# Second routing of a two-layer MoE chain: expert logits from four column strips of the array and one product with a 0-1 matrix

## The chip, the core and the metric

One NeuronCore of a Trainium2 chip runs the whole program. The metric is the device time of one execution in microseconds (us), less is better. The engines are TensorE (PE; its weight loads are listed as PEld), VectorE (DVE), ScalarE (ACT), GpSimd (POOL) and SyncE (SP, which here only issues DMAs). Each engine works through its own queue in program order.

## The reference, cut to what matters

```python
def reference(...):
    attn_out = _attn_ref(q, k, v)               # decaying linear attention, 2 x 8 heads x 768 tokens x 64
    x = attn_out.transpose(0, 2, 1, 3).reshape(1536, 512)
    x = _moe_ref(x, w_skip, w_gate, w1, w2)     # tokens with x @ w_skip > 0 go to 1 of 8 experts
    return _moe2_ref(x, w_gate2, w1b, w2b, capacity)

def _moe2_ref(x, w_gate, w1, w2, capacity):
    logits = x @ w_gate                         # 1536 x 8
    expert_idx = np.argmax(logits, axis=1)
    ...                                         # place of each token within its expert, softmax gate
    h = np.maximum(np.einsum('ecd,edf->ecf', disp, w1), 0.0)
    y = np.einsum('ecf,efd->ecd', h, w2)
    ...                                         # out[i] = gate_w[i] * y[expert_idx[i], pos[i]]
```

All data are float32; there are 1536 tokens of 512 features, 8 experts and 1024 hidden features in both MoE layers.

## The kernel before, in words

The program has three stages on the same core: the attention with the routing of the first MoE, the first MoE with the routing of the second, and the second MoE. A block is 128 tokens on 128 partitions; 512 features are four parts (`KT` = 4) of 128. An expert's weights come in four chunks of 1 MB (two of layer 1, two of layer 2) through `load_w`; `prep` makes of each chunk a rounded copy `hi` on ACT (L236, a copy of 128x2048) and a remainder `lo` on DVE (L244). A product with such weights (`mm3`, L680 to L682) is three matmuls, hi x hi, hi x lo and lo x hi.

The order of the work in the second stage is written out by hand. The loop at L827 goes over the experts e. In each turn there are `layer1` of expert e (24 matmuls of 512 columns), the turning of the next block x (`split_T`, four transposes at L673, then L383 on ACT and L384 on DVE), `layer2` of expert e-1 (24 matmuls) and the turning of the hidden block h (eight transposes). The generators yield after every six matmuls and after every four transposes. At each yield `run` calls `step_side`, which lets every side generator do its next piece; so one turn has eleven side steps. `prep` is called at four places in a turn: at its start, in the middle of `layer1` (right after the relu of its first half, L696 to L698), after the turning of x, and in the middle of `layer2`.

`route_b` (L713) is the side generator that routes the finished block of expert e-1 for the second MoE. `then_route` starts it after `layer2` with a number of idle steps ahead (`lead`) and a number of idle steps after the logits (`rest`). Its pieces are:

- start: the new rows `r2` on DVE (L716), and some small ones (L721, L723)
- with lead 3, at the second side step of the next turn (in the middle of the next `layer1`): four transposes (L731) into a PSUM bank, and a copy of 128x512 by ACT into `x2t` (L733)
- one step later: `token_logits` (L248), four products with the feature part of `x2t` as the 128-column weights and 8 gate columns of `idw` as the moving side; then `pick` (L284: a chain of eight small DVE operations from L289 to L309, with Exp on ACT, L296), the write of the rows to the table by a DMA on POOL's queue (L344), and `mrow` (L741) on DVE
- `1 + rest` steps later: `ranked` (two bf16 products), `prb`, `slb`, `hotb` (L746, L748, L378) and `cumb` on DVE
- one step later: one product of `hotb` and `mrow` (L758) and the sum into `idb` (L759); for e = 6 also the gather of the first block of the second MoE and `load_held`

The steps on ACT around it, in program order, are: L733, the relu of the first half of `layer1` (L696), `hi` of a weight chunk (L236), Exp (L296), the relu of the second half (L696), `xh` of the next block (L383), the next `hi`.

`then_route` is called for the blocks 0 to 5 with lead 3 and rest 3, for block 6 with lead 3 and rest 1, and for block 7 (the last, with no loop turn behind it) with lead 0 and rest 1. `idw[:, g, :]` holds, of feature parts 2g and 2g+1, the 17 gate columns of the odd part in columns 0 to 16, a 128x128 identity in 17 to 144, and the 17 gate columns of the even part in 145 to 161; the second MoE's gate columns are the entries 8 to 15 of the 17. `psum()` gives one of three banks by turns. `constants` (L127) sets up small constants on POOL before the second chunk of the attention.

```python
        x2t = m_p.tile([128, KT, 128], F32, tag="x2t", name="x2t", bufs=1)
        nc.scalar.activation(out=x2t, in_=xr.rearrange("p (k t) -> p k t", k=KT), func=ACTF.Copy)
        yield
        lp = psum()
        token_logits(lp, lambda k: x2t[:, k, :], 8, 8)
        m = pick(lp[:, 0:8].unsqueeze(1), 1, 1, rm, ...)[:, 0, :]
```

Of the kernel before, what the change touches and what calls it, by code (L numbers as in the profile page):

```python
# [7 lines left out]
F32 = mybir.dt.float32  # L8
# [3 lines left out]
ACTF = mybir.ActivationFunctionType  # L12
ALU = mybir.AluOpType
# [3 lines left out]
NT, DM, E, FF = B * S, H * D, 8, 1024  # L17
NCH = S // 128
NTILE = NT // 128
KT = DM // 128  # L20
# [13 lines left out]
C_ID = C_GS + 4 * NCH  # L34
# [11 lines left out]
def kernel(  # L46
# [12 lines left out]
    nc = tc.nc  # L59
    ctx.enter_context(tc.manual_schedule())  # L60
    const = ctx.enter_context(tc.tile_pool(name="const", bufs=1))
# [11 lines left out]
    def bank(name, *tags):  # L73

        i = turns[name] = turns.get(name, -1) + 1
        tag = tags[i % len(tags)]
        return ps.tile([128, 512], F32, tag=tag, bufs=BANKS[tag], name=name)
# [17 lines left out]
    cs = const.tile([128, C_N], F32, name="cs")  # L95
# [3 lines left out]
    idw = const.tile([128, 2, 164], F32, name="idw")  # L99
# [9 lines left out]
    iota = const.tile([128, 256], F32, name="iota")  # L109
    idacc = const.tile([128, 2, 16], F32, name="idacc")  # L110
    idb = const.tile([128, E], F32, name="idb")

    def no_rows():

        nc.sync.dma_start(out=table[0:1, :], in_=zb[0:1, :].bitcast(F32))
# [11 lines left out]
    def constants():  # L127
        nc.sync.dma_start(out=cs[:, C_ID:C_N], in_=cst[:, C_ID:C_N])
        wk = wg.rearrange("p (g i) n -> p g i n", i=2)
        nc.sync.dma_start(out=idw[:, :, 145:162], in_=wk[:, :, 0, 0:17])  # L130
        nc.sync.dma_start(out=idw[:, :, 0:17], in_=wk[:, :, 1, 0:17])
        nc.sync.dma_start(out=cap_i, in_=capacity.bitcast(I32))
        for t in t9.values():
            nc.gpsimd.memset(t, 0.5)
        for g in range(2):
            nc.gpsimd.tensor_copy(out=idw[:, g, 17:145], in_=cs[:, C_ID:C_ID + 128])
        nc.gpsimd.tensor_copy(out=lc, in_=cs[:, C_L:C_L + 256].rearrange("p (a t) -> p a t", a=2))
        nc.gpsimd.tensor_copy(out=iota[:, 0:128], in_=cs[:, C_IOTA:C_IOTA + 128])
        nc.gpsimd.tensor_scalar(out=iota[:, 128:256], in0=cs[:, C_IOTA:C_IOTA + 128], scalar1=128.0, scalar2=None, op0=ALU.add)
        nc.gpsimd.memset(cum, 0.0)  # L140
        nc.gpsimd.memset(cumb, 1.0)
        nc.gpsimd.memset(idacc, 0.0)
        nc.gpsimd.tensor_copy(out=cap, in_=cap_i[:, 0:1])
        for t in row2:
            nc.gpsimd.memset(t, 0.0)

    def idle(n):
        for _ in range(n):
            yield
# [39 lines left out]
    def load_held():  # L189

        held[1] = True
        for _ in range(held[0]):
            load_w()
# [54 lines left out]
    def token_logits(lp, xk, c0, n):  # L248

        for k in range(KT):  # L250
            w0 = c0 + (0 if k % 2 else 145)
            nc.tensor.matmul(out=lp[:, 0:n], lhsT=xk(k), rhs=idw[:, k // 2, w0:w0 + n], start=k == 0, stop=k == KT - 1)  # L252

    def xk(rows, k):

        return rows[:, KW * k:KW * k + 128]

    def x_all(rows):
        return rows.rearrange("p (k z) -> p k z", z=KW)[:, :, 0:128]
# [57 lines left out]
    def ranked(rk, lmat, m2d, cum2d):  # L317
        n = m2d.shape[-1]
        nc.tensor.matmul(out=rk[:, 0:n], lhsT=lmat, rhs=m2d, start=True, stop=False)
        nc.tensor.matmul(out=rk[:, 0:n], lhsT=ones, rhs=cum2d, start=False, stop=n < 32)  # L320
        if n == 32:
            nc.tensor.matmul(out=rk[:, 16:32], lhsT=ones, rhs=m2d[:, 0:16], start=False, stop=True)
# [15 lines left out]
    def write_rows(eng, src, n, c0=0, c1=RW):  # L338

        r0 = done[0]  # L340
        r1 = r0 + 128 * n
        if c1 == RW:
            done[0] = r1
        eng.dma_start(out=table[r0:r1, c0:c1].rearrange("(n p) w -> p n w", p=128), in_=src[:, :, c0:c1])  # L344
# [21 lines left out]
    def places(out, rank, m0):  # L366

        n = rank.shape[-1]
        sl = sm.tile([128, n], F32, tag=f"sl0{n}", name="sl0")
        nc.vector.scalar_tensor_tensor(out=sl, in0=m0, scalar=-AWAY, in1=rank, op0=ALU.mult, op1=ALU.add)  # L370
        for i in range(n):
            nc.vector.tensor_scalar(
                out=out[:, i, :], in0=iota[:, 0:128], scalar1=-AWAY, scalar2=sl[:, i:i + 1], op0=ALU.add, op1=ALU.is_equal
            )

    def slot_hot(out, rank):

        nc.vector.tensor_scalar(  # L378
            out=out, in0=iota[:, 0:out.shape[-1]], scalar1=rank, scalar2=None, op0=ALU.is_equal
        )  # L380
# [268 lines left out]
    def psum(name="t"):  # L649
        return bank("e" + name, *{"t": "a", "s": "cbb", "o": "d"}[name])  # L650
# [62 lines left out]
    def route_b(e, xs, acc, lead, rest):  # L713

        r2 = row2[e % 2]
        nc.vector.scalar_tensor_tensor(  # L716
            out=x_all(r2), in0=acc.rearrange("p (k t) -> p k t", k=KT), scalar=xs[:, GCOL:GCOL + 1], in1=x_all(xs),
            op0=ALU.mult, op1=ALU.add,
        )
        if xs is not r2:  # L720
            nc.vector.tensor_copy(out=r2[:, IDCOL:IDCOL + 1], in_=xs[:, IDCOL:IDCOL + 1])  # L721
        rm = sm.tile([128, 1, 8], F32, tag="rmb", name="rmb")
        nc.vector.scalar_tensor_tensor(  # L723
            out=rm, in0=xs[:, IDCOL:IDCOL + 1].unsqueeze(1).to_broadcast([128, 1, 8]), scalar=0.0, in1=rev.unsqueeze(1),
            op0=ALU.not_equal, op1=ALU.mult,
        )
        yield
        yield from idle(lead)
        xr = psum()
        for k in range(KT):  # L730
            nc.tensor.transpose(xr[:, 128 * k:128 * k + 128], xk(r2, k), ident)  # L731
        x2t = m_p.tile([128, KT, 128], F32, tag="x2t", name="x2t", bufs=1)
        nc.scalar.activation(out=x2t, in_=xr.rearrange("p (k t) -> p k t", k=KT), func=ACTF.Copy)  # L733
        yield
        lp = psum()
        token_logits(lp, lambda k: x2t[:, k, :], 8, 8)
        m = pick(lp[:, 0:8].unsqueeze(1), 1, 1, rm, r2[:, GCOL + 1:GCOL + 2].unsqueeze(1))[:, 0, :]
        write_rows(nc.gpsimd, r2.unsqueeze(1), 1)
        n = NTILE + e
        mrow = sm.tile([128, E], F32R, tag="mrowb", name="mrowb")  # L740
        nc.vector.tensor_scalar(out=mrow, in0=m, scalar1=cs[:, C_ROW + n:C_ROW + n + 1], scalar2=None, op0=ALU.mult)  # L741
        yield from idle(1 + rest)
        rk = psum()
        ranked(rk, lc[:, 1, :], m, cumb)
        pr = sm.tile([128, E], F32, tag="prb", name="prb")
        nc.vector.tensor_tensor(out=pr, in0=rk[:, 0:8], in1=m, op=ALU.mult)  # L746
        sl = sm.tile([128, 1], F32, tag="slb", name="slb")
        nc.vector.tensor_reduce(out=sl, in_=pr, axis=AX.X, op=ALU.add)  # L748
        hot = sm.tile([128, 128], F32R, tag="hotb", name="hotb", bufs=1)
        slot_hot(hot, sl)  # L750
        nc.vector.tensor_tensor(out=cumb, in0=cumb, in1=m, op=ALU.subtract)
        if e == E - 1:
            oh = sm.tile([128, 128], F32, tag="ohb", name="ohb", bufs=2)
            places(oh.unsqueeze(1), sl, m[:, 0:1])
            late.append((r2, oh))
        yield
        new = psum()
        nc.tensor.matmul(out=new[:, 0:E], lhsT=hot, rhs=mrow, start=True, stop=True)  # L758
        nc.vector.tensor_tensor(out=idb, in0=idb, in1=new[:, 0:E], op=ALU.add)  # L759
        if e == E - 2:  # L760
            late.append(gather(numbers(idb[:, 0:1], "id0"), 1 + NT + 128 * E - 128))
            load_held()
        yield
# [58 lines left out]
    def then_route(e, acc, lead, rest):  # L822
        g = route_b(e, xs1[e], acc, lead, rest)
        next(g)
        side.append(g)

    for e in range(E):  # L827
        if e > 1:
            prep()
        h = run(layer1(x, "w1a", e, prep))  # L830
        if e + 4 < E:
            xs1[e + 4] = gather(ida[:, e + 4:e + 5], 1 + NT)
        elif e == 4:
            gather(ida[:, 8:9], 1 + NT, a0)
        turn = split_T(h, FT, "hT")
        if e == 0:
            next(turn)
        x = run(split_T(xs1[e + 1] if e + 1 < E else a0, KT, "x"))
        prep()
        if e:  # L840
            acc = run(layer2(hT.pop(e - 1), "w2a", e - 1, prep))
            then_route(e - 1, acc, 3, 3 if e < E - 1 else 1)
        hT[e] = run(turn)
    prep()
    acc = run(layer2(hT.pop(E - 1), "w2a", E - 1, prep))
# [31 lines left out]
    acc = run(layer2(h0, "w2b", 0))  # L877
# [59 lines left out]
    acc = run(layer2(h0, "w2b", 0, prep))  # L937
# [202 lines left out]
```

## Time and profile before

| | |
|---|---|
| three runs, median (lowest to highest) | 396.01 us (395.87 to 396.07) |
| the profiled execution, its own time | 394.56 us |
| its span, first to last instruction | 392.8 us |
| PE busy | 376.2 us, 96% of the span, 2605 matmuls |
| DVE busy | 259.7 us, 66% |
| ACT busy | 215.6 us, 55% |
| POOL busy | 69.9 us, 18% |
| granted clock of TensorE, mean | 0.994 of full speed |

The second stage, with the code of the change, runs from about 80 to 208 us of the span. In the turn from 118.29 to 132.60 us PE is busy for 14.28 of 14.31 us, DVE for 13.30 and ACT for 10.79. The matmuls overlap in the records (a new one starts while the former still drains), so the cost of a group of matmuls is read from its start to the start of the next group, not from its busy time. One float32 product shows as two matmul records; a transpose and a product with a float32r operand as one. Instructions on ACT and DVE overlap by about 0.1 us in the same way.

### The profile page before, as it was taken

The page shows a single profiled execution, that of the slowest core. Times are in us where ns is not written, and L with a number is a line of the kernel's source. Part 1 is how long each engine was busy: PE and PEld are TensorE (multiplying, and loading weights), DVE is VectorE, ACT ScalarE, POOL GpSimd, SP SyncE. Part 2 cuts the span into 40 slices and gives each one's busy share as a digit, 9 for nine tenths or more (in the row PEclk, how much of TensorE's full clock was granted, in tenths as well). Part 3 has the DMA queues.
Part 4 walks back from the last instruction along what each step waited for, and adds up shares of the span by engine and source line. Part 5 has one row for each costly group of instructions (what it writes and reads, how often), then busy time and mean ns, then how long its engine had stood idle before and what let it go on. Part 6 is the DMA issues. An engine that isn't in the chain of part 4 may idle for free.

```text
span 392.8 us, 6614 instructions
## 1 busy us (share of the span) xinstructions
PE 376.2 (96%) x2605; PEld 321.0 (82%) x2605; DVE 259.7 (66%) x476; ACT 215.6 (55%) x283; POOL 69.9 (18%) x97
## 2 busy tenths in 40 slices
PE   8899989899999999999999999999999999999992
PEld 3788878678877877877778898989989899898981
DVE  2668986478898999999863868383574738455210
ACT  1557773296778777777543845545545555552201
POOL 6310010180031010000026020404013040301101
PEclk9999999999999999999999999999999999999997
DMA  8999993489999999889875587858575684320101
GB/s 304 402 419 417 379 333 120 131 298 385 391 351 336 343 357 316 323 319 300 333 260 159 180 283 236 279 164 306 168 230 191 224 288 136 130 62 7 47 2 41
DMA packets 18409, 97.69 MB, mean 249 GB/s; under 512 B 3263, under 2 KB 3391, under 8 KB 8900
## 3 DMA queue, kind: packets, MB, share of 16 engines
q1 hardware_dynamic: 12180, 80.03, 56.5%
q0 software_dynamic: 4000, 13.25, 10.1%
q10 hardware_dynamic: 2192, 3.93, 2.7%
q8 instruction: 22, 0.36, 0.3%
q14 instruction: 15, 0.12, 0.1%
HBM read 88.11 MB, written 10.14 MB: 250 GB/s over the span
## 4 chain that ended last, share of the span: by engine, by line
PE 71%; DVE 10%; issue 7%; ACT 6%; DMA 5%; POOL 1%; POOLq 0%; ACTq 0%; DVEq 0%
PE eo L680 10%; PE es L680 10%; PE es L682 10%; PE es L681 10%; PE eo L682 10%; PE eo L681 9%; DMA cs<-in_cst_dram 4%; DVE lo L244 3%; PE s L267 2%; PE et L673 2%; ACT hi L236 2%; DVE lo L228 2%; PE et L252 1%; PE et L890 1%; DMA a<-table,id 1%
## 5 line engine op out<-in xcount | busy, mean ns | idle before, releaser
L244 DVE TENSOR_TENSOR lo<-raw,hi 128x2048 fp32r<-128x2048 f32 x60 | 136.2, 2283 | 5.9 <-ACT hi L236 5.9
L236 ACT ACTIVATE hi<-raw 128x2048 fp32r<-128x2048 f32 x60 | 114.7, 1915 | 20.2 <-PE eo L682 15.4
L680 PE MATMUL eo<-hi,hTh 128*128 128x512 f32 x192 | 77.9, 406 | 0.2 <-ACT hTh L383 0.2
L682 PE MATMUL eo<-hi,hTl 128*128 128x512 f32 x192 | 75.5, 393 | 0.0
L681 PE MATMUL eo<-lo,hTh 128*128 128x512 f32 x192 | 75.0, 390 | 0.0
L682 PE MATMUL es<-xh,lo 128*128 128x256 f32 x224 | 62.9, 281 | 0.0
L680 PE MATMUL es<-xh,hi 128*128 128x256 f32 x224 | 62.9, 281 | 0.0
L681 PE MATMUL es<-xl,hi 128*128 128x256 f32 x224 | 62.9, 281 | 0.0
L910 DVE SCALAR_TENSOR_TENSOR hTl<-es,hTh 128x512 fp32r<-128x512 f32 x28 | 19.3, 691 | 63.1 <-ACT hTh L909 63.1
L325 POOL DMA_INDIRECT out_dram<-y,ixo x16 | 20.2, 1260 | 142.3 <-ACT y L767 129.5
L682 PEld LDWEIGHTS eo<-hi,hTl 128*128 128x128 f32 x192 | 36.0, 188 | 8.5 <-DVE hTl L384 0.5
L681 PEld LDWEIGHTS es<-xl,hi 128*128 128x128 f32 x224 | 42.7, 191 | 0.3
L680 PEld LDWEIGHTS es<-xh,hi 128*128 128x128 f32 x224 | 42.7, 190 | 0.3
L682 PEld LDWEIGHTS es<-xh,lo 128*128 128x128 f32 x224 | 42.7, 191 | 0.0
L680 PEld LDWEIGHTS eo<-hi,hTh 128*128 128x128 f32 x192 | 36.1, 188 | 6.9 <-ACT hTh L383 0.5
L681 PEld LDWEIGHTS eo<-lo,hTh 128*128 128x128 f32 x192 | 36.2, 188 | 6.8
L909 ACT ACTIVATE hTh<-es 128x512 fp32r<-128x512 f32 x28 | 16.7, 598 | 40.0 <-PE es L682 40.0
L680 PE MATMUL es<-hi,xh 128*128 128x512 f32 x80 | 33.4, 418 | 0.3 <-ACT xh L383 0.3
L682 PE MATMUL es<-hi,xl 128*128 128x512 f32 x80 | 31.6, 395 | 0.1
L681 PE MATMUL es<-lo,xh 128*128 128x512 f32 x80 | 31.3, 392 | 0.0
L767 ACT ACTIVATE y<-eo,xs 128x512 f32<-128x512 f32 x15 | 10.3, 688 | 33.0 <-PE eo L682 25.2
L540 DVE TENSOR_TENSOR p<-s,cs 128x512 f32<-128x512 f32 x24 | 15.4, 682 | 12.7 <-PE s L531 12.7
(153 smaller groups left out, 506.0 us busy)
## 6 DMA issues: line engine op xcount, KB each, us to landing
raw<-in_w1a_dram SPq DMA_DIRECT2D x16, 1024.0 KB, 7.0
raw<-in_w2a_dram SPq DMA_DIRECT2D x16, 1024.0 KB, 7.1
raw<-in_w1b_dram SPq DMA_DIRECT2D x16, 1024.0 KB, 5.2
raw<-in_w2b_dram SPq DMA_DIRECT2D x16, 1024.0 KB, 4.9
ain<-in_qkv_dram SPq DMA_DIRECT2D x10, 1024.0 KB, 10.1
table<-rowc ACTq DMA_DIRECT2D x5, 580.0 KB, 5.8
table<-row POOLq DMA_DIRECT2D x8, 290.0 KB, 6.6
ain<-in_qkv_dram SPq DMA_DIRECT2D x4, 512.0 KB, 5.8
```

The lines of the kernel that those rows point to most:

```text
L228: nc.vector.tensor_tensor(out=lo[:, k], in0=r3[:, k], in1=hi[:, k].bitcast(F32), op=ALU.subtract)
L236: nc.scalar.activation(out=hi, in_=r3, func=ACTF.Copy)
L244: nc.vector.tensor_tensor(out=lo, in0=r3, in1=hi.bitcast(F32), op=ALU.subtract)
L267: nc.tensor.matmul(out=t[:, 128 * i:128 * i + KW], lhsT=xt(2 * g + i), rhs=idw[:, g, 17 - 17 * i:17 - 17 * i + KW], start=i == 0, stop=i = ...
L325: return nc.gpsimd.indirect_dma_start(out=dst[:, :], out_offset=bass.IndirectOffsetOnAxis(ap=idx, axis=0), in_=src, in_offset=None, bounds ...
L540: nc.vector.tensor_tensor(out=t, in0=sa[j].rearrange("p (r t) -> p r t", r=4), in1=mask.unsqueeze(1).to_broadcast([128, 4, 128]), op=ALU.mult,
L680: nc.tensor.matmul(out=acc, lhsT=a[0], rhs=w[0], start=first, stop=False)
L681: nc.tensor.matmul(out=acc, lhsT=a[0], rhs=w[1], start=False, stop=False)
L682: nc.tensor.matmul(out=acc, lhsT=a[1], rhs=w[0], start=False, stop=last)
L767: nc.scalar.activation(out=y, in_=acc, func=ACTF.Copy, scale=xs[:, GCOL + 1:GCOL + 2])
L909: nc.scalar.activation(out=hi[:, g:g + 2, :], in_=acc, func=ACTF.Relu)
L910: nc.vector.scalar_tensor_tensor(out=lo[:, g:g + 2, :], in0=acc, scalar=0.0, in1=hi[:, g:g + 2, :].bitcast(F32), op0=ALU.max, op1=ALU.subtract
```

## The change

In `route_b`, for the blocks 0 to 6, the logits are made in another way. Each of the four feature parts gets its own product, with 32 columns of `idw` as the weights and the 128 tokens of `x2t` as the moving side; the outputs go to four strips of 32 partitions of one PSUM bank. The 32 columns start at 0 for an odd part and at 130 for an even one, so that they hold the 8 gate columns of the second MoE and other columns. ACT copies the 128x128 result over the first part of `x2t`, and after a further side step one product with this copy as weights and a 128x8 matrix `sel` as the moving side adds the four strips' gate rows and turns the result to tokens on partitions. `sel` is 1 where a row of the strips is gate row j; POOL builds it in `constants` from the identity. The idle steps after the logits are one fewer for the blocks 0 to 5. Block 7 keeps the old way.

```diff
+    sel = const.tile([128, E], F32, name="sel")
...
         nc.gpsimd.memset(idacc, 0.0)
+        nc.gpsimd.tensor_copy(out=sel, in_=cs[:, C_ID + 23:C_ID + 31])
+        for z in (40, 87, 104):
+            nc.gpsimd.tensor_tensor(out=sel, in0=sel, in1=cs[:, C_ID + z:C_ID + z + 8], op=ALU.add)
...
         yield
         lp = psum()
-        token_logits(lp, lambda k: x2t[:, k, :], 8, 8)
+        if e == E - 1:
+            token_logits(lp, lambda k: x2t[:, k, :], 8, 8)
+        else:
+            for k in range(KT):
+                w0 = 0 if k % 2 else 130
+                nc.tensor.matmul(
+                    out=lp[32 * k:32 * k + 32, 0:128], lhsT=idw[:, k // 2, w0:w0 + 32], rhs=x2t[:, k, :], start=True, stop=True
+                )
+            nc.scalar.activation(out=x2t[:, 0, :], in_=lp[:, 0:128], func=ACTF.Copy)
+            yield
+            lp = psum()
+            nc.tensor.matmul(out=lp[:, 0:8], lhsT=x2t[:, 0, :], rhs=sel, start=True, stop=True)
         m = pick(lp[:, 0:8].unsqueeze(1), 1, 1, rm, r2[:, GCOL + 1:GCOL + 2].unsqueeze(1))[:, 0, :]
...
-            then_route(e - 1, acc, 3, 3 if e < E - 1 else 1)
+            then_route(e - 1, acc, 3, 2 if e < E - 1 else 1)
```

## Rows read from the trace of the kernel before

**Rows 1.** Part 1 of the page: busy time, share of the span, instructions.

```profile
PE 376.2 (96%) x2605; PEld 321.0 (82%) x2605; DVE 259.7 (66%) x476; ACT 215.6 (55%) x283; POOL 69.9 (18%) x97
```

**Rows 2.** Timeline, PE, routing of block 1: start us, duration us, engine, line.

```profile
117.96 0.60 PE L731 MATMUL et<-cs,row 128*128 128x128 f32 x4
...
119.81 0.95 PE L252 MATMUL et<-idw,x2t 128*128 128x8 f32 x8
120.61 0.48 PE L680 MATMUL es<-hi,xh 128*128 128x512 f32 x1
...
122.11 0.60 PE L673 MATMUL et<-cs,xs 128*128 128x128 f32 x4
```

**Rows 3.** Timeline, ACT, the same stretch; idle time before and its releaser in brackets.

```profile
118.66 0.60 ACT L733 ACTIVATE x2t<-et 128x512 f32<-128x512 f32 x1 [0.86 <-PE et L731]
119.15 0.59 ACT L696 ACTIVATE h<-es 128x512 f32<-128x512 f32 x1
119.63 1.91 ACT L236 ACTIVATE hi<-raw 128x2048 fp32r<-128x2048 f32 x1
121.55 0.21 ACT L296 ACTIVATE ex<-d 128x8 f32<-128x8 f32 x1
122.31 0.60 ACT L696 ACTIVATE h<-es 128x512 f32<-128x512 f32 x1 [0.56 <-PE es L682]
```

**Rows 4.** Timeline, DVE, the same stretch, to the hot matrix of block 1.

```profile
121.15 0.16 DVE L289 TENSOR_REDUCE mx<-et 128x1 f32<-128x8 f32 x1
...
122.48 0.21 DVE L741 TENSOR_SCALAR mrowb<-m,cs 128x8 fp32r<-128x8 bf16 x1
123.43 0.69 DVE L384 TENSOR_TENSOR xl<-et,xh 128x512 fp32r<-128x512 f32 x1 [0.74 <-ACT xh L383]
...
126.63 0.29 DVE L378 TENSOR_SCALAR hotb<-iota,slb 128x128 fp32r<-128x128 f32 x1
```

**Rows 5.** Timeline, PE: the product with the hot matrix, and block 2's transposes.

```profile
127.06 0.24 PE L758 MATMUL et<-mrowb,hotb 128*128 128x8 f32 x1
...
132.25 0.60 PE L731 MATMUL et<-cs,row 128*128 128x128 f32 x4
```

**Rows 6.** Waits, 100 to 208 us: who waited, total us, times, longest us.

```profile
PEld et L758 <- PE eo L682: 3.4, 6, 1.1
```

**Rows 7.** Groups by line and form, ACT: count, busy us, mean ns, idle before.

```profile
L296 ACT ACTIVATE ex<-d 128x8 f32<-128x8 f32 x8 | 1.7, 209 | 2.1 <-DVE d L294 1.5
...
L383 ACT ACTIVATE xh<-m 128x256 fp32r<-128x256 f32 x2 | 0.8, 384 | 5.2 <-PE m L361 5.2
```

**Rows 8.** Timeline, block 0: a PE wait that ends with an ACT copy.

```profile
104.00 0.60 ACT L733 ACTIVATE x2t<-et 128x512 f32<-128x512 f32 x1
...
104.65 0.97 PEld L252 LDWEIGHTS et<-idw,x2t 128*128 128x128 f32 x8 [0.57 <-ACT x2t L733]
```

**Rows 9.** Timeline, PE, attention stage: full array, then two strips of 64 partitions.

```profile
54.30 1.16 PE L570 MATMUL m<-ain,sbd 128*128 128x128 f32 x8
55.39 1.09 PE L580 MATMUL m<-p,ain 128*64 128x128 f32 x16
56.42 0.19 PE L319 MATMUL s<-m,lc 128*128 128x32 bf16 x1
```

**Rows 10.** Timeline, blocks 6 and 7, around the end of the second stage.

```profile
191.42 1.90 ACT L236 ACTIVATE hi<-raw 128x2048 fp32r<-128x2048 f32 x1
...
192.06 0.95 PE L252 MATMUL et<-idw,x2t 128*128 128x8 f32 x8
...
193.05 0.17 DVE L289 TENSOR_REDUCE mx<-et 128x1 f32<-128x8 f32 x1 [0.30 <-PE et L252]
...
194.54 0.75 DVE L716 SCALAR_TENSOR_TENSOR row<-eo,xs 128x512 f32<-128x512 f32 x1
...
195.78 0.63 PE L731 MATMUL et<-cs,row 128*128 128x128 f32 x4
```

**Rows 11.** Timeline, POOL, start of the program.

```profile
22.30 0.56 POOL L438 TENSOR_TENSOR cum<-cum,m 128x32 bf16<-128x32 bf16 x2 [3.77 <-PE s L322]
```

## The prediction

> **What bounds the kernel now.** I read part 1 of the page first: PE is busy for 96% of the span [rows 1], so it looks as if any PE time saved in the routing came off the end. Then I read the timelines of one routing in the second stage, block 1, engine by engine, because the change puts a second engine between two PE pieces. On PE the reader sees the transposes at 117.96, the eight logit records from 119.81 to the next matmul at 120.61, and the six matmuls of a side step up to the next group at 122.11 [rows 2]. The logits thus cost 0.80 us, and the step behind them 1.50 us. On ACT stand the copy to `x2t`, a relu, a weight copy `hi` of 1.91 us up to 121.54, then Exp and the second relu [rows 3]. On DVE the small chain of `pick` starts at 121.15 and `xl` waits 0.74 us for ACT's `xh` [rows 4].
>
> The row to look at longest is L758. The hot matrix starts on DVE at 126.63 and L758 at 127.06, 0.43 us later [rows 4, 5]. The list of waits has PE's weight load for L758 idle six times, 3.4 us in all, behind a PE instruction that had long been done [rows 6]; what L758 really reads is the hot matrix. I measured the same 0.43 us in all five routings of blocks 1 to 5. So PE, busy as it is, already waits once in each turn for a chain that runs from the transposes over ACT and DVE: `x2t`, relu, `hi` | logits | `pick`, Exp, relu, `xh` | `xl`, a weight remainder, rank, hot matrix, L758. From L758 to the next transposes (127.06 to 132.25) [rows 5] PE alone sets the pace. A turn lasts as long as this chain and that stretch together, 14.29 us from transposes to transposes [rows 2, 5].
>
> **The change part by part, for block 1.**
>
> *The strips.* Removed are 0.80 us of logits [rows 2]. Added are eight records of 128 moving columns. In the full array eight such cost 1.09 us (54.30 to 55.39); on two strips sixteen cost 1.03 (55.39 to 56.42), so 0.064 each and 0.51 for eight [rows 9]. Four strips at best halve that again, 0.26. The ends are 0.26 and 1.09; I take 0.4, between the best case and the two-strip row, which is nearest. The Trainium skill (TensorEngine Tiling (Array Packing), Key Properties) says that a change of tiling mode drains the engine; by that rule the strips would lie nearer 0.51 than 0.26, and the sum would stay the same, for the reason that follows.
>
> *The copy, and what it stands behind.* The side step with the strips comes after the middle of `layer1`, so ACT's copy is behind the relu and the `hi` of that place in ACT's queue. `hi` starts at 119.63 and takes 1.91; the next ACT instruction can start about 0.11 before it ends, as `hi` itself does against the relu (119.15 + 0.59 = 119.74) [rows 3]. So the copy starts at 121.43. A copy of 128x128 lies between 0.21 (8 columns) and 0.38 (256) [rows 7]; by the line through both it is 0.29. It ends at 121.72, and a product that waits for an ACT copy starts 0.05 later (104.60 to 104.65) [rows 8]: 121.77. PE gets there at 119.81 + 0.4 + 1.50 = 121.71 [rows 2]. So up to 0.46 us of strips are hidden by ACT, and the PE time saved is given back as a wait. Behind the product on PE stand only x's transposes; two records at 0.10 each and the start put them at 122.1, where they are now.
>
> *The pick.* Now `mx` follows the product. Where `mx` waited for the logits, it came 0.99 us after the first of eight records (192.06 to 193.05) [rows 10]; less six at 0.10 that is 0.39, with the weights loaded ahead, which a waiting product can't do. Between 0.39 and 0.99 I take 0.5. So `mx` moves from 121.15 to 122.27. DVE had nothing to wait for here; now it idles, with `xl` and the next weight remainder queued behind. Exp comes 0.40 after `mx`, the second relu 0.10 behind Exp (0.21 less the overlap), and `xl` 1.12 after that relu [rows 3, 4]: 122.27 + 0.40 + 0.10 + 1.12 = 123.89. DVE's own chain ends at 122.27 + 1.33 + 0.21 = 123.81, so ACT decides. Against 123.43 `xl` is 0.46 late, and so are the remainder, the hot matrix and L758. PE waits for it and the turn gets 0.46 longer.
>
> *The sum.* In blocks 1 to 5 the stretch has the same form within some hundredths: 5 x 0.46 = 2.3. In block 0 DVE is late already, so the added wait lies between nothing and 0.46; I take 0.2.
>
> Block 6 keeps its rest of 1, so here its logits, rank, L758, gather and `load_held` all come one step later. ACT is free by 193.55 there (191.42 + 1.90 - 0.11 + 0.29 + 0.05), and PE arrives at 192.06 + 0.4 + 1.50 = 193.96, so `mx` comes at 194.35 instead of 193.05 [rows 10]. Behind that `pick` DVE has block 7's `r2` (L716): 194.54 + 1.30 = 195.84, done at 196.59, and block 7's transposes, at 195.78 now, can't start before 196.64: 0.9 us lost. The gather and `load_held` move by 1.5 us; the block is used in a place behind block 7's own chain, and the loads are five buffers ahead, so I cost them at nothing; uncovered they would cost those 1.5 us once.
>
> POOL's four operations for `sel` at some 0.28 each (two took 0.56) fit in an idle time of 3.77 us [rows 11]; without it they would delay the first rows by 1.1 us. POOL's row writes follow `pick` by the same 1.1 us; behind them are gathers that are used three turns later, so I cost that at nothing, and if they were needed it would be 1.1 once. The extra PSUM bank is one whose reader is done turns of three earlier; nothing.
>
> Together 2.3 + 0.2 + 0.9 = 3.4 us. The profiled execution would go from 394.56 to 398.0; the median of the runs shown is 1.45 above that execution, so I predict 399.4. Lower end of this case: strips at 0.26 and a copy that is never late give a product at 121.57, `mx` at 121.96 and 0.15 per block, with 0.6 at the end of the stage: 1.4 us, 397.4. Upper end: `mx` at 0.99 after the product adds 0.5 in five blocks, 2.5 more: 401.9.
>
> **Rivals.**
>
> *Faster.* If L758 doesn't set the turn, the 0.43 us being only a coincidence of a busy queue, and ACT's copy isn't late, PE keeps what it saves: 0.80 less 0.4 (or 0.26) less 0.20 for the product, 0.2 to 0.34 in seven blocks, so 1.4 to 2.4 us: 394.2. It decides if PE reaches L758 after the hot matrix. For it speaks PE's 96% [rows 1]; against it the six waits [rows 6], and that even with a free ACT `mx` comes later than now. The Trainium skill (the same page, Theoretical Speedup) promises up to four times for a dimension of at most 32, which is this case's hope; it would need PE to be what is waited for.
>
> *No change.* The product's wait eats the saving, but what DVE loses is taken up by some slack on the way to L758 that I don't see: 396.0. Against it: DVE is busy from `xl` on without a gap.
>
> *Strips one after another.* At 1.09 us PE reaches the product at 122.40, `mx` is at 122.79 and `xl` 0.98 late: 5 x 0.98 + 0.5 + 1.6 = 7.0, 403.0. The change would then not do what it says. The two-strip rows speak against it.
>
> **How the numbers follow.** Some 0.2% is what a measurement of this kernel can tell from no change, 0.8 us. My case has 0.80, the strips in series 0.05, so slower 0.85; no change 0.06; faster 0.09. The range for the time takes my case, from what is just measurable (396.8) to 401.6 near its upper end, and leaves out the others, 0.20.
>
> **What would show it.** Right: in the timeline of block 1 a product behind the ACT copy, whose weight load waits for `x2t`; the copy starting as the `hi` ends; `mx` idle about 1 us before it, released by the product; L758 still 0.43 us behind the hot matrix, and PE's wait there some 0.5 longer; transposes to transposes 14.75 us instead of 14.29. Block 7's transposes wait for `r2`. Wrong: a turn of 14.1 us or less, no idle DVE ahead of `mx`, or a copy that starts well before `hi` is done. The strips' cost is read from their first start to the next matmul.

## The result, and the profile after

The changed kernel takes 399.18 us (median of four runs, 398.44 to 399.72) against 396.04 us before on the same chip. The ratio is 1.0085, with a 95% interval of 1.0066 to 1.0104, so it is slower by 3.1 us. The profiled execution took 398.44 us, with a span of 396.6 us against 392.8.

The first part of the profile's page says almost nothing of it: PE is busy for 376.6 us instead of 376.2 [rows 1] and the span is 3.8 us longer. The lost time is idle time.

```profile
PE 376.6 (95%) x2619; PEld 316.8 (80%) x2619; DVE 260.5 (66%) x476; ACT 215.7 (54%) x290; POOL 74.4 (19%) x101
```

From the transposes of block 0 to the last sums of the second stage it is 107.99 us before (102.52 to 210.51) and 111.01 after (102.83 to 213.84). So 3.02 of the 3.8 us lie in the stage that was changed. Another 0.31 lie ahead of it, 0.23 of them from a DMA of constants that landed later in this execution, and the rest in one turn of the last stage, which is shorter than its neighbours in the one profiled execution of before. The last stage holds no instruction of the change. The start holds POOL's four operations for `sel`, but the 0.23 arose before them (POOL's wait for these constants ends at 15.66 us instead of 15.43), and POOL still idles for 2.80 us behind them, where it was 3.77. The medians differ by 3.14.

The timeline of PE in the routing of block 1, to set beside [rows 2] and [rows 5]. L747 are the strips, L753 the product with the 0-1 matrix, L735 the transposes and L775 the product with the hot matrix:

```profile
118.25 0.60 PE L735 MATMUL et<-cs,row 128*128 128x128 f32 x4
...
119.89 0.39 PE L686 MATMUL es<-hi,xl 128*128 128x512 f32 x1
120.21 0.42 PE L747 MATMUL et<-x2t,idw 128*32 128x128 f32 x8
120.56 0.50 PE L684 MATMUL es<-hi,xh 128*128 128x512 f32 x1
...
122.06 0.37 PE L753 MATMUL et<-sel,x2t 128*128 128x8 f32 x2
122.29 0.64 PE L677 MATMUL et<-cs,xs 128*128 128x128 f32 x4
...
126.84 0.40 PE L686 MATMUL eo<-hi,hTl 128*128 128x512 f32 x1
127.72 0.24 PE L775 MATMUL et<-mrowb,hotb 128*128 128x8 f32 x1 [0.49 <-DVE cumb L768]
...
132.94 0.60 PE L735 MATMUL et<-cs,row 128*128 128x128 f32 x4
```

The strips take 0.36 us where the old logits took 0.80 [rows 2]. The turn is nevertheless 14.69 us instead of 14.29. ACT in the same stretch, beside [rows 3]:

```profile
119.92 1.92 ACT L240 ACTIVATE hi<-raw 128x2048 fp32r<-128x2048 f32 x1
121.72 0.27 ACT L750 ACTIVATE x2t<-et 128x128 f32<-128x128 f32 x1
122.88 0.21 ACT L300 ACTIVATE ex<-d 128x8 f32<-128x8 f32 x1 [0.88 <-DVE d L298]
```

The copy of the strips (L750) starts as the weight copy ends, 1.16 us after the next matmul on PE shows the strips to be over. DVE, beside [rows 4]:

```profile
122.47 0.17 DVE L293 TENSOR_REDUCE mx<-et 128x1 f32<-128x8 f32 x1 [0.94 <-PE et L753]
...
124.09 0.69 DVE L388 TENSOR_TENSOR xl<-et,xh 128x512 fp32r<-128x512 f32 x1
...
127.29 0.29 DVE L382 TENSOR_SCALAR hotb<-iota,slb 128x128 fp32r<-128x128 f32 x1
```

DVE, which went from a weight remainder straight to `mx` before, now waits 0.94 us for the product. `mx` comes 4.22 us after the transposes instead of 3.19, `xl` 5.84 instead of 5.47. L775 is 0.43 us behind the start of the hot matrix, exactly as before. The list of waits, 100 to 212 us (who waited for whom: us, times, longest), beside [rows 6]:

```profile
DVE mx L293 <- PE et L753: 5.9, 6, 1.5
PEld et L775 <- PE eo L686: 5.4, 6, 0.9
```

The weight load for the hot product, 3.4 us in all before, is idle for 5.4 us. The end of the stage, blocks 6 and 7, beside [rows 10]:

```profile
196.29 0.28 PE L753 MATMUL et<-sel,x2t 128*128 128x8 f32 x2
...
198.96 0.63 PE L735 MATMUL et<-cs,row 128*128 128x128 f32 x4 [0.90 <-DVE rmb L727]
```

Block 7's transposes stand 6.43 us behind block 6's (192.53) instead of 5.55, and 0.90 us of that is a wait for DVE.

### The profile page after: what moved, and what is told of

Same layout as the page of the kernel before. It is cut to its first block, busy times and chain, and to the rows that moved or that the text cites. A ratio compares the mean times of both kernels' runs of the same rounds, so it can differ in the third digit from the quotient of the medians.

```text
span 396.6 us, 6655 instructions
## 1 busy us (share of the span) xinstructions
PE 376.6 (95%) x2619; PEld 316.8 (80%) x2619; DVE 260.5 (66%) x476; ACT 215.7 (54%) x290; POOL 74.4 (19%) x101
## 4 chain that ended last, share of the span: by engine, by line
PE 61%; DVE 13%; DMA 10%; issue 7%; ACT 6%; POOL 1%; POOLq 0%; ACTq 0%; DVEq 0%; SPq 0%
PE es L684 9%; PE es L685 9%; PE es L686 9%; PE eo L684 8%; PE eo L686 8%; PE eo L685 7%; DVE lo L248 5%; DMA cs<-in_cst_dram 4%; DMA raw<-in_w1a_dram 3%; DMA ain<-in_qkv_dram 2%; PE s L271 2%; PE et L677 2%; DVE lo L232 1%; ACT hi L240 1%; PE et L907 1%
```

## The experiments

There were eight runs, of seven kernels. The question was whether the loss is the late `pick`, as forecast, or TensorE's own: the strips, the other tiling, the extra product.

**The old logits, one step later.** The kernel before, with nothing of the change but the delay:

```diff
         yield
+        if e < E - 1:
+            yield
         lp = psum()
         token_logits(lp, lambda k: x2t[:, k, :], 8, 8)
...
-            then_route(e - 1, acc, 3, 3 if e < E - 1 else 1)
+            then_route(e - 1, acc, 3, 2 if e < E - 1 else 1)
```

> The kernel before, with its old logits products, only one side step later for blocks 0 to 6 (one idle step after the copy to x2t, one fewer after the logits). No strips, no copy, no 0-1 product. Theory of the chain (a later pick makes the hot matrix late, and PE waits for it at its product): in blocks 1 to 5 the old products start about 3.2 us after the transposes instead of 1.85, mx comes 4.2 us after the transposes as in the changed kernel (4.22) instead of 3.2, a turn is 14.6 to 14.7 us, block 7's transposes wait about 0.9 us, and the time is 399.0 us (398.5 to 399.6). Rival (the loss is TensorE's own: strips, the change of tiling, the extra product and its wait for ACT): all of that is absent here, so 396.0 us (395.7 to 396.4).

It took 398.64 us, ratio 1.0068 (1.0047 to 1.0089). Timelines of PE and DVE, block 1:

```profile
119.64 0.60 PE L731 MATMUL et<-cs,row 128*128 128x128 f32 x4
...
122.88 0.96 PE L252 MATMUL et<-idw,x2t 128*128 128x8 f32 x8
123.87 0.17 DVE L289 TENSOR_REDUCE mx<-et 128x1 f32<-128x8 f32 x1 [0.94 <-PE et L252]
...
128.68 0.29 DVE L378 TENSOR_SCALAR hotb<-iota,slb 128x128 fp32r<-128x128 f32 x1
...
129.11 0.24 PE L760 MATMUL et<-mrowb,hotb 128*128 128x8 f32 x1 [0.49 <-DVE cumb L753]
```

`mx` comes 4.23 us after the transposes, DVE waits the same 0.94 us, the turns of blocks 1 to 4 are 14.65 to 14.70 us, and block 7's transposes wait 0.90 us. From the transposes of block 0 to the last sums of the stage it is 111.09 us (104.19 to 215.28), against 111.01 in the changed kernel and 107.99 before. So in the profiles the loss of the stage is there in full without a strip, a copy or a second product. The times alone would not say in full: 2.6 us here and 3.1 there, with intervals that overlap. The rival, which gave 396.0 us, falls.

**The hot product one step later, in both kernels.** The wait at the end of the chain is taken away by giving the chain six matmuls more:

```diff
+        if e < E - 2:
+            yield
         new = psum()
         nc.tensor.matmul(out=new[:, 0:E], lhsT=hot, rhs=mrow, start=True, stop=True)
```

In the kernel before:

> The kernel before, with the product of the hot matrix one side step (six matmuls, 1.4 us) later for blocks 0 to 5. Theory of the chain: the kernel before waits at this product already, about 0.2 us in each of five turns (0.43 us behind the hot matrix each time) and some 0.7 us in block 0; both go, a turn falls from 14.29 to about 14.1 us and the time to 394.3 us (394.0 to 395.3). Rival (PE alone sets the turn, the 0.43 us is a coincidence): the same work in another order, 396.0 us.

In the changed kernel:

> The changed kernel, with the product of the hot matrix one side step later for blocks 0 to 5. Theory of the chain: the wait of about 0.65 us at this product goes in blocks 0 to 5, a turn falls from 14.69 to about 14.05 us, and the time falls by up to 3.9 us to 395.3 us (395.0 to 396.5); what stays is the 0.9 us at block 7. Rival (TensorE's own costs): nothing of the strips is touched, 399.2 us.

They took 393.37 us (ratio 0.9937, 0.9917 to 0.9956) and 394.98 us (0.9973, 0.9954 to 0.9993). Transposes of blocks 1 and 2, first in the kernel before with the step, then in the changed one with it:

```profile
119.49 0.60 PE L731 MATMUL et<-cs,row 128*128 128x128 f32 x4
...
133.45 0.60 PE L731 MATMUL et<-cs,row 128*128 128x128 f32 x4
```

```profile
117.34 0.60 PE L735 MATMUL et<-cs,row 128*128 128x128 f32 x4
...
131.23 0.60 PE L735 MATMUL et<-cs,row 128*128 128x128 f32 x4
```

The turn falls from 14.29 to 13.96 us in the one and from 14.69 to 13.89 in the other. The second fall is the larger, as it must be if both kernels waited at this product and the changed one waited longer. With the wait gone the order is turned round: in these turns the strips now save 0.07 us. The first kernel gained 0.13 us more in each turn than I expected (14.29 to 13.96, not to 14.1). I had counted the 0.2 us by which L758 starts late. The product itself now also takes 0.03 us to the next PE instruction (129.74 to 129.77) instead of 0.10 (127.06 to 127.16), which is about half of the 0.13; no run separates the rest.

The step does not help in the turn from block 5's transposes to block 6's: it is 15.14 us in the kernel before with the step and without it, and 15.53 in the changed kernel with and without it. What PE waits for there is shown below.

**The old logits for block 6 too.**

```diff
-        if e == E - 1:
+        if e >= E - 2:
             token_logits(lp, lambda k: x2t[:, k, :], 8, 8)
```

> The changed kernel, with the old logits for block 6 as well as for block 7. Theory: block 6's pick, and behind it on DVE block 7's rows, come as early as before; block 7's transposes no longer wait for them (0.90 us idle in the changed kernel), so 0.9 us less: 398.3 us (398.0 to 398.6). Rival (TensorE's own costs): one block in seven less, so about a seventh of 3.1 us, 398.7 us, with the idle time ahead of block 7's transposes still there.

It took 398.15 us, ratio 1.0047 (1.0025 to 1.0070), 1.0 us below the changed kernel but with runs from 396.4 to 400.0, so the time alone would not decide between 0.9 and 0.5. The transposes of blocks 6 and 7 do:

```profile
195.09 0.60 PE L735 MATMUL et<-cs,row 128*128 128x128 f32 x4
...
200.64 0.64 PE L735 MATMUL et<-cs,row 128*128 128x128 f32 x4
```

They are 5.55 us apart, as before, and the wait of 0.90 us is gone; the four turns between blocks 1 and 5 stay at 14.66 to 14.76.

**No step between strips and product.**

```diff
             nc.scalar.activation(out=x2t[:, 0, :], in_=lp[:, 0:128], func=ACTF.Copy)
-            yield
             lp = psum()
...
-            then_route(e - 1, acc, 3, 2 if e < E - 1 else 1)
+            then_route(e - 1, acc, 3, 3 if e < E - 1 else 1)
```

> The changed kernel without the side step between the strips and the 0-1 product: the product follows the strips at once, and the idle steps after it are 3 again for blocks 0 to 5. Theory (ACT's copy stands behind the weight copy of that place and ends 3.7 us after the transposes): PE waits about 1.4 us at the product with everything behind it, mx comes no earlier than in the changed kernel (4.2 us after the transposes), and the second half of layer 1 and with it xh, xl and the hot matrix come 1.0 us later still; a turn is about 15.7 us and the time 405.4 us (403.5 to 406.5). Rival (the copy is free as soon as the strips are done, the lateness is the side step's alone): PE waits about 0.6 us, mx comes 3.3 us after the transposes, about as in the kernel before, a turn is 14.3 to 14.8 us and the time 396 to 399 us.

The ratio is 1.0259 (1.0226 to 1.0293), which of 395.75 us for the kernel before is 406.0 us. Timelines of PE and ACT, block 1:

```profile
120.87 0.60 PE L735 MATMUL et<-cs,row 128*128 128x128 f32 x4
...
122.83 0.43 PE L747 MATMUL et<-x2t,idw 128*32 128x128 f32 x8
124.67 0.39 PE L752 MATMUL et<-sel,x2t 128*128 128x8 f32 x2 [1.42 <-ACT x2t L750]
...
136.54 0.60 PE L735 MATMUL et<-cs,row 128*128 128x128 f32 x4
```

```profile
122.54 1.91 ACT L240 ACTIVATE hi<-raw 128x2048 fp32r<-128x2048 f32 x1
124.34 0.28 ACT L750 ACTIVATE x2t<-et 128x128 f32<-128x128 f32 x1
```

The copy again starts where the weight copy ends and PE waits 1.42 us for it, 1.45 in four further blocks. `mx` (125.10) comes 4.23 us after the transposes, no earlier than with the step, and the turn is 15.67 us. So the queue on ACT is why the step was needed, and why `pick` comes no earlier with it or without it as long as the copy stands behind that weight copy. No run put the copy on another engine or ahead of the weight copy. The profiled execution also had one turn of 17.22 us among these, of which more below.

**Both waits away, with strips and without.** The changed kernel with the later hot product and the old logits for block 6, and the kernel before with the later hot product once more, on one chip:

> The changed kernel with the product of the hot matrix one side step later for blocks 0 to 5 and the old logits for block 6. Theory: neither PE's wait for the hot matrix nor block 7's wait for its rows is left, PE alone sets the turn at 13.90 us, and the strips keep what they save on PE, about 0.07 us in a turn against the kernel before with the same later product: 393.3 us (392.8 to 394.2), within 0.2% of that kernel. Rival (the copy or the strips cost something that the turns don't show): as the changed kernel with the later product alone, 395.0 us.

> The kernel before with the product of the hot matrix one side step later, once more, to stand beside the one with strips on the same chip: 393.4 us (392.9 to 394.0), turns of 13.96 us; its earlier profiled execution had 1.4 us more in block 0, ahead of the logits, which is not expected here.

They took 393.81 us (ratio 0.9957, 0.9940 to 0.9973) and 394.42 us (0.9956, 0.9936 to 0.9977). The 1.4 us in block 0 did not come again; in that earlier execution a weight DMA landed later, PE waited 1.06 us for ACT at the logits of block 0, and behind that the granted clock was 0.50 from 107 to 110 us. One turn of each in the stretches view (length, then busy us of PE, PEld, DVE, ACT, POOL, granted clock, DMA), with strips first:

```profile
117.58:131.47 13.89, 13.89 (x78) 10.93 (x77) 13.40 (x25) 10.74 (x12) 3.38 (x2) 1.00 0.93 326
```

```profile
118.99:132.95 13.96, 13.96 (x77) 11.59 (x75) 13.48 (x25) 10.81 (x11) 3.52 (x2) 1.00 0.97 357
```

PE has no idle time in either turn, and with the strips it is 0.07 us shorter. That holds for the four turns between blocks 1 and 5. The next one, to block 6's transposes, is 15.54 us with the strips (173.16 to 188.70) and 15.14 without (174.82 to 189.96). PE's longest wait in it, with strips first:

```profile
186.29 0.50 PE L686 MATMUL eo<-hi,hTl 128*128 128x512 f32 x1 [0.89 <-DVE hTl L388]
```

```profile
187.54 0.50 PE L682 MATMUL eo<-hi,hTl 128*128 128x512 f32 x1 [0.45 <-DVE hTl L384]
```

The remainder `hTl` of the turned hidden block is made on DVE behind `pick`, `xl`, two weight remainders and the next block's new rows: `xl` starts 5.84 us after the transposes with the strips and 5.44 without, `hTl` 12.39 and 11.99. So the later `pick` still costs 0.40 us in this turn, by a second way to PE, and the expectation that no wait is left was wrong here. In block 0, too, PE still waits for ACT with the strips, 0.31 us ahead of them and 0.44 at the product. Four times 0.07 us does not make up for the 0.40. The two times differ by 0.6 us with intervals that are wider, and the earlier measurement of the second kernel is below both. By the ratios both beat the kernel before by some 1.7 us; that one of them beats the other is not shown.

**The strips twice.** The kernel with both waits away, and the four strip products done twice:

```diff
-            for k in range(KT):
+            for k in list(range(KT)) * 2:
```

> The same with strips, later product and old logits for block 6, but with all four strip products of blocks 0 to 5 done twice (the second time over the first, same result). Theory (PE now sets the turn, four strips run at the same time, about 0.034 us a record): eight records more cost 0.27 us in each of six blocks, a turn goes from 13.90 to 14.17 us, 394.9 us (394.4 to 395.6). Rivals: strips two at a time, 0.51 us each and 396.4 us; strips one after another, 1.09 us each and 399.8 us; strips hidden under a wait for ACT, 393.3 us.

It took 394.57 us, ratio 0.9980 (0.9964 to 0.9996). PE's timeline in block 1, once (the kernel with both waits away) and twice:

```profile
119.53 0.42 PE L747 MATMUL et<-x2t,idw 128*32 128x128 f32 x8
119.89 0.50 PE L684 MATMUL es<-hi,xh 128*128 128x512 f32 x1
...
121.39 0.38 PE L753 MATMUL et<-sel,x2t 128*128 128x8 f32 x2
121.62 0.63 PE L677 MATMUL et<-cs,xs 128*128 128x128 f32 x4
```

```profile
119.72 0.64 PE L747 MATMUL et<-x2t,idw 128*32 128x128 f32 x16
120.29 0.50 PE L684 MATMUL es<-hi,xh 128*128 128x512 f32 x1
...
121.79 0.29 PE L753 MATMUL et<-sel,x2t 128*128 128x8 f32 x2
121.94 0.63 PE L677 MATMUL et<-cs,xs 128*128 128x128 f32 x4
```

Eight records more take 0.21 us (0.57 less 0.36), 0.026 a record, a quarter of the 0.10 of an old logits record. So the four strips do run at the same time. The turn rises by 0.10 us only, from 13.90 to 13.99 on the average of four, not by 0.27: beside the smaller price, the product takes 0.15 instead of 0.23 us when PE comes later, since part of it was a wait for ACT's copy. Both rivals of slower strips fall, and so does my own theory's claim that PE alone was left.

## Why the prediction was right

The forecast was 399.4 us and the time 399.18, for the reason given: the first experiment gives the loss with the delay alone, and the next two take it away, in the four turns between blocks 1 and 5, at the wait that was named. That the two numbers agree to 0.2 us is partly luck. The stage lost 3.02 us and not 3.4; 0.78 us of the longer span lie outside it and were not forecast; and the median lies 0.74 us above the profiled execution, where 1.45 was taken over from the kernel before. By its steps:

- *The strips.* Taken at 0.4 us; they take 0.36, and the first starts 0.32 us after the matmul ahead of it where 0.23 is usual, so 0.45 with the entry. The Trainium skill (TensorEngine Tiling (Array Packing), Key Properties) says that a change of tiling mode drains the engine; the 0.09 us agree with it, and the first weight load of the strips also starts only at 120.20, but no run separates a drain from another cost of entry. The same page of the Trainium skill (Theoretical Speedup) gives up to four times for 32 columns; the 0.026 us of a further strip record, a quarter of the 0.10 of an old logits record, agree with it. The cheaper products brought nothing here, because PE was not what was waited for.
- *The copy.* Forecast to start 3.47 us after the transposes, to take 0.29, and to let the product start at 3.81. Measured: 3.47, 0.27 and 3.81.
- *The saving given back.* I had it as a wait at the product. PE reaches the product just as the copy is done, so there is next to none there; it is given back at the hot product, where PE would be ready at 127.07 (126.84 and the usual 0.23) and starts at 127.72: 0.65 us instead of about 0.2.
- *`mx` and the turn.* `mx` comes 0.41 us after the product and not 0.5. This is the term that was mis-sized. It makes 0.40 us in a turn instead of 0.46: the transposes of blocks 1 and 6 lie 74.28 us apart instead of 72.27, 2.01 more where 2.3 was forecast. That all five turns have one form was a misreading: the fifth is 15.14 us before, and in it the lateness reaches PE by `hTl` too, as the experiments show. That it lost 0.39 us, nearly as much as the others, is luck.
- *Block 0.* Taken at 0.2; it is nothing (15.42 us to the next transposes instead of 15.44). DVE is there still the later one, and `mx` does not wait.
- *Block 6 and 7.* Forecast 0.9; measured 0.88, and the fourth experiment shows whose wait it is. Some 0.15 us more come behind it, which were not forecast.
- *The edits costed at nothing.* The gather of block 6 goes out 3.35 us later than before, no more than the whole stage is late, and its use does not wait. POOL's four operations at the start have no one behind them that waits.

The sum forecast for the stage was 3.4 us; 2.01 + 0.88 + 0.15 - 0.02 = 3.02 were found. The faster rival needed the 0.43 us between hot matrix and product to be a coincidence; it stayed at 0.43 to 0.44 in the changed kernel and in the three experiments that leave the hot product in its place (blocks 1 to 5).

## What to carry to other kernels

An engine that is busy for 96% of the span can still be led by a chain over two others: look for a fixed distance between a producer's start on one engine and the consumer's on the busy one, repeated turn by turn. Before an instruction is moved a step later in an order written by hand, follow what comes out of it to the next such place, and look at what stands ahead of it in each queue; here a small copy behind a large one cost more than the products that it allowed to be cheaper. Where the wait is found, giving the consumer more room was worth 2.6 and 1.3 us of the median in two measurements of the kernel before, and only with that room did the cheaper products save anything, 0.07 us in each of four turns, while the fifth still lost 0.40. A late chain can have more than one consumer: look for the next wait behind the one that was taken away.

## What the runs showed of the hardware

The kernel without the step between strips and product had a turn of 17.22 us among turns of 15.65 to 15.70. The stretch behind the product of block 3, in the same view as above:

```profile
155.99:159.51 3.52, 3.52 (x12) 2.84 (x13) 1.35 (x9) 0.68 (x2) 0.58 (x1) 0.56 1.01 410
```

The granted clock is 0.56 there, that is mostly at 1.2 instead of 2.4 GHz, and matmuls that are otherwise 0.23 us apart are 0.43 apart; then it rises again. Ahead of it PE had waited 1.42 to 2.03 us at the product of each of four blocks. In block 0 of the same execution it fell too, to 0.50 from 109 to 112 us, behind the wait of 2.03. Why it fell in these two blocks and not in the others with waits of 1.42 and 1.45, the runs do not show. Falls also stand in the two profiles of the kernel before with the later hot product: 0.50 from 107 to 110 us in the first, behind a wait of 1.06 us at the logits of block 0, and 0.80 and 0.78 over 76 to 80 and 80 to 84 us in the second. They are part of the spread of 1 to 2 us between runs of one kernel: in the second measurement of that kernel the two runs with a mean granted clock of 0.998 took 393.16 and 393.30 us, the ten with 0.989 to 0.993 took 393.98 to 395.00. That is why the turns are compared here beside the times.
